# Chunk attention and a gelu MLP in one kernel: two more indices with a second block of seven products, totals of both halves in one set, and another order of mm1's steps

## The chip, the cores and the metric

The kernel runs on one core of a Trainium2 chip. A core has TensorE (matrix products, called PE in a profile, with its weight loads as PEld), VectorE (DVE), ScalarE (ACT), GpSimd (POOL) and SyncE (SP, which here only issues DMAs). Each engine takes its instructions in the order in which the program lists them for it, and waits where a semaphore is not there yet. Matrix products go from SBUF to PSUM, which has eight banks. The metric is the device time of one execution in microseconds.

## The reference

Attention is done within chunks of 64 keys, and its result is the input of a two-layer MLP with an exact gelu. Sizes: 8 batches, 8 heads, 576 positions, 64 per head; 4608 tokens, width 512, inner width 2048.

```python
scores = scale * np.matmul(q_c, k_c.transpose(0, 1, 2, 4, 3))     # per chunk of 64
attn = np.exp(scores - max) / (sum + 1e-09)
x = (attn @ v_c) ...transposed to (B * S, H * D)                   # 4608 x 512
h = x @ w_in                                                       # 512 x 2048
g = 0.5 * h * (1.0 + erf(h / sqrt(2)))
out = g @ w_out                                                    # 2048 x 512
```

## The kernel before

**Tiling.** The rows are cut into nine tiles of 512, called indices 0 to 8 (`t` in the code, `NT = 9`). Index t below 8 holds the first eight chunks of batch t; index 8 holds the ninth chunk of all batches. The loop `for t in range(1, NT)` does, in `phase(t, ...)`, the MLP of index t, and in between the attention of index n = t + 1, and starts that of index t + 2. `mm1` is x times w_in with the gelu; `mm2` is the product with w_out.

**mm1.** Its output, h, has 16 row blocks (128 inner columns of w_in each, 512 tokens wide). A *slot* makes one of them: four 128x512 matmuls (L463) into one bank of the pool `ps_mm`, and a gelu on ScalarE (L465). Four row blocks together can also be made by *seven products* in place of eight (`seven_rows`): the 2x2 block product of (512 x 512) w_in with x is formed by Strassen's scheme in Winograd's form. A product is four 128x256 matmuls (L536), `p1` to `p7`. It needs sums of blocks of x (`x_sums`, VectorE, L519) and of w_in (`w_in_sums`, VectorE, L513; set 0 for row blocks 0 to 3, set 1 for 4 to 7). The combining steps are `s11` (ScalarE copies p1 from bank a to bank b, L549), p5's copy to SBUF (L548, `kept`), `s12` and `c22+` (VectorE adds, L540) and the gelus `c11`, `c12`, `c22` and p3's own (L544). Banks a, b and d are shared: p6, p7 and p3 write over bank a, which `s12` and `c22+` read. Indices in `TWICE` (5 to 8) make row blocks 4 to 7 in this way too; those steps carry a prime (`p1'`), have banks a and b in the pool `ps_tp`, and take bank b of the first block as their d. The order of steps, slots (numbers) and hooks of an index is a tuple written out by hand in `mm1_seven`.

**mm2.** `mm2_seven` makes the 512 x 512 output of an index by seven products of 32 matmuls 128x256 (L683). It needs sums of blocks of h on VectorE: S1, S2, S4 in two parts each (`g_sum`, L621), and S3 (L608). Hook `g0` does the first parts, `s3` the third sum, and the second parts stand in mm2's hook 0 and 2. S1 and S2 lie in the memory that holds the sums of x during mm1. The results of the products are kept by ScalarE (L645), completed by VectorE (`done`, L650) and stored by SyncE.

**Attention of the next index.** `quad_S` makes the scores (64 small matmuls, L237), ScalarE the exponentials (L244), `quad_av` the products with v (L327). Sums of the exponentials: for indices 3 and 4 by a TensorE product with ones (`quad_sums`), spread by ScalarE copies (`quad_over`) and VectorE transposes; for indices 5 to 8 by VectorE alone: `quad_part` (L254, L257), then totals over pairs of quadrants, reciprocals and transposes (`quad_total`, `quad_rc`; L283 to L293). `quad_x_plain` (L320) and `quad_x` (L334) scale the result and give x of the next index.

**k by chunk.** For the scores, k is transposed by a DMA (`flip`, L194, tile k_t), which SyncE issues in its queue between loads and stores, and then copied to another layout (`k_by_chunk`, L205, four copies to tile k_c, which has one buffer): on VectorE for indices 3, 4 and 5, on ScalarE for the later ones. Where these copies stand among VectorE's other work is given by the hook that they hang on. In index 2 (for index 3) it was in front of slot 10, in index 3 (for index 4) in front of slot 8; in index 3 a second set (for index 5) hangs on slot 15 and has to wait until the scores of index 4 have read the only buffer.

**Start.** Before the first data are there, TensorE runs matmuls on zeros: three of 128x512, and `pass_blocks(108)`, 108 products of 64x64 by 64x8 (L821).

Of the kernel before, what the change touches and what calls it, by code (L numbers as in the profile page):

```python
# [11 lines left out]
def kernel(  # L12
# [9 lines left out]
    nc = tc.nc  # L22
    P = 128
    f32 = mybir.dt.float32
# [4 lines left out]
    CH = 64  # L29
# [3 lines left out]
    G = H // 2  # L33
# [5 lines left out]
    NT = B + 1  # L39
# [21 lines left out]
    QD = P // G  # L61
# [27 lines left out]
    work = ctx.enter_context(tc.tile_pool(name="work", bufs=3))  # L89
# [158 lines left out]
    def quad_part(t, g2, c):  # L248

        st = tiles[t]  # L250
        if c == 1:
            st["part", g2] = work.tile([P, 2, NB // 2, 2, 2], f32, tag="part", name="part", bufs=2)
        pt = work.tile([P, NB // 2, 32, 2], bf16, tag="pt", name="pt", bufs=2)
        nc.vector.transpose(  # L254
            pt[:].rearrange("p n e u -> p (n e u)").bitcast(f32).rearrange("p (n e) -> p n e", e=32),
            st["pT", 2 * g2 + c][:].rearrange("p i c -> p (i c)").bitcast(f32).rearrange("p (n e) -> p n e", e=32))
        nc.vector.tensor_reduce(st["part", g2][:, c, :, :, 0], pt[:].rearrange("p n e u -> p n u e"),  # L257
                                axis=mybir.AxisListType.X, op=mybir.AluOpType.add)

    def quad_across(t):  # L260

        part = [tiles[t]["part", g2] for g2 in range(2)]
        for g2 in range(2):
            for s in range(G):
                o = s ^ 1
                PO(part[g2][QD * s:QD * (s + 1), :, :, :, 1], part[g2][QD * o:QD * (o + 1), :, :, :, 0])

    def quad_total(t, halves=range(2)):

        part = [tiles[t]["part", g2] for g2 in range(2)]  # L270
        if 0 in halves:
            tiles[t]["across"] = [work.tile([P, NB], f32, tag="across", name="across", bufs=2) for _ in range(2)]
        across = tiles[t]["across"]
        for g2 in halves:
            total, rb = (work.tile([P, 2, NB], f32, tag=nm, name=nm, bufs=2) for nm in ("total", "rb"))
            if t == T0 + 2:
                nc.vector.tensor_reduce(total[:], part[g2][:].rearrange("p c n u s -> p c (n u) s"),
                                        axis=mybir.AxisListType.X, op=mybir.AluOpType.add)
            else:
                for s in range(G):  # L280
                    a, b = (part[g2][QD * q:QD * (q + 1), :, :, :, 0].rearrange("p c n u -> p c (n u)")
                            for q in (s, s ^ 1))
                    nc.vector.tensor_tensor(total[QD * s:QD * (s + 1)], a, b, op=ADD)  # L283
            nc.vector.reciprocal(rb[:, 0], total[:, 0])
            tiles[t]["rb", g2] = rb[:, 0], across[g2][:]
            if g2 == 0:
                quad_rc(t, 0, 0)
            for r in range(2):
                nc.vector.reciprocal(across[g2][CH * r:CH * (r + 1)], total[CH * (1 - r):CH * (2 - r), 1])  # L289

    def quad_rc(t, g2, c):
        rc = work.tile([P, NB, 32], f32, tag="rc", name="rc", bufs=4)
# [129 lines left out]
    NB = MT // 32  # L422
# [44 lines left out]
    NQ = 4  # L467
    T0 = 3
    DENSE = (0, 1)
    TWICE = range(T0 + 2, NT)  # L470

    HF = FF // 2
    HD = d_model // 2
# [87 lines left out]
    def mm1_seven(t, hooks):  # L561

        tiles[t]["h"] = hpool.tile([P, FF, MT], bf16, tag="h", name="h")
        kept = stage_tile()[:].rearrange("p (i f n) -> p i f n", f=HM, n=HD)
        bank, more = {}, {}
        does = seven_rows(t, 0, {"a": AT, "b": AT, "d": AT}, kept[:, 0], bank)
        if t in TWICE:
            does.update((step + "'", do) for step, do in
                        seven_rows(t, 1, {"a": TP, "b": TP}, kept[:, 1], more).items())
            fifth = does["p5'"]  # L570
            does["p5'"] = lambda: (more.update(d=bank["b"]), fifth())
        if t == NT - 1:
            order = ("p1", "s11", "p1'", "s11'", "p5", 8, "p2", "c11", "p6", 9, "s12", "p5'", "p6'", "s12'", 10, "p7", "p4",
                     "c22+", "c12", "c22", "p7'", 11, "p3", "p2'", "c11'", "c22+'", "p4'", "c22'", 12, "c12'", "p3'", 13,
                     "g0", 14, "s3", 15)
        elif t in TWICE:
            order = ("p1", "s11", "p5", 8, "p2", "p1'", "t0", "c11", "s11'", 9, "p5'", "p6", 10, "p6'", 11, "s12", "p7",
                     "s12'", "p7'", "p4", "c12", "c22+", "c22+'", "p2'", "c11'", "p4'", "t1", "c22", 12, "p3", "p3'",
                     "c12'", "c22'", 13, "g0", 14, "s3", 15)
        elif t == T0 + 1:  # L580
            order = ("x", 4, 5, 6, "p1", "s11", 7, "p5", "p2", "c11", "p6", 8, "s12", "t0", 9, "p4", "p7", "c12", "c22+", "t1",
                     10, "c22", 11, "p3", 12, "s3", 13, "g0", 14, 15)
        elif t == T0:
            order = ("x", "p1", "s11", 4, "p5", "p2", "c11", 5, "p6", "s12", 6, "p4", "p7", "c12", "c22+", 7, "c22", 8, "p3",
                     9, 10, "s3", 11, 12, 13, "g0", 14, 15)
        else:
            order = ("x", 4, 5, 6, "p1", "s11", 7, "p5", "p2", "c11", 8, "p6", "s12", 9, "p4", "p7", "c12", "c22+", 10, "c22",
                     11, "p3", 12, "s3", 13, "g0", 14, 15)
        for step in order:
            if step in does:  # L590
                does[step]()
                continue
            for u in hooks.get(step, ()):
                u()
            if not isinstance(step, str):
                mm1_slot(t, step)
# [232 lines left out]
    with tc.manual_schedule():  # L829
# [4 lines left out]
        win = [load_w_in(c, 2) for c in range(NWC - 1)]  # L834
        act_table(Act.Exp)
        keep_warm(3)
        pass_blocks(108)
        zero_k(k_bds[0], nc.gpsimd)
        zero_k(k_bds[1], nc.gpsimd)
        zero_v(0, nc.vector)  # L840
# [114 lines left out]
        for t in range(1, NT):  # L955
# [40 lines left out]
            if t <= T0:  # L996
# [2 lines left out]
                e2 = {0: [exp, lambda: quad_S(n, ALONE)] + g[1][:2], 2: g[1][2:],  # L999
                      4: [lambda: quad_sums(n)], 5: [ov[0]], 6: [ov[1]],  # L1000
                      7: [ov[2]] + rx[0], 8: [ov[3]] + rx[1], 9: rx[2], 10: rx[3]}
                e2[7 if t == 1 else 4].insert(1, lambda: quad_av(n, ALONE))
                if t > 1:
                    e1["x"] = [lambda: x_sums(t)]
                if t == 2:
                    e1[13] = [lambda: w_in_sums(1)]
                if t == 1:
                    e2[3] = [w_in_sums]
                    for i, f in ((1, 6), (2, 7), (3, 8), (4, 9)):
# [1 line left out]
                    e2[4].append(lambda: [load_qk(4, nm) for nm in "qk"])  # L1011
                    e2[7] += [lambda: pool_cast_qk(4), lambda: flip_qk(3), lambda: load_v_rows(3), lambda: cast_v_rows(3, PO)]
                else:
                    e1[10 if t < T0 else 8] = [lambda: k_by_chunk(n, DV)]
                if t < T0:
                    if t > 1:
                        e2[0].append(lambda: flip_qk(n + 1))
# [7 lines left out]
            elif n < NT:  # L1025
# [3 lines left out]
                    e1["t0"] = [lambda: quad_total(n, (0,))]  # L1029
                    e1["t1"] = [lambda: quad_total(n, (1,)), rcs[1]]  # L1030
                else:
                    e1["t0"] = [lambda: quad_total(n)]
                    e1["t1"] = rcs[1:]
                e2 = {0: [exp, lambda: quad_av(n, ALONE)] + xs[:2] + g[1][:2], 4: xs[2:] + g[1][2:],
                      6: [lambda: x_sums(n, (0, 1))], 10: [lambda: x_sums(n, (2, 3))], 11: [gelu]}
                if t == T0 + 1:
                    e2[0] = e2[0][:2] + g[1][:2] + xs[:2]
                    e2[2] = rcs[2:]
                if n + 1 < NT:
                    for i, gs in enumerate(((0,), (1, 2), (3,))):  # L1040
# [32 lines left out]
```

## Time and profile before

| | us |
|---|---|
| median of 3 runs (lowest, highest) | 275.51 (275.08, 276.24) |
| profiled execution | 275.01 |
| its span, first to last instruction | 273.2 |
| TensorE, VectorE, ScalarE, GpSimd busy | 263.5, 204.8, 192.8, 89.9 |
| index 2 (mm1 and mm2), from 78.72 to 106.85 | 28.1 |
| index 3, from 106.85 to 135.52 | 28.7 |
| index 4, from 135.52 to 163.04 | 27.5 |
| index 5, from 163.04 to 190.21 | 27.2 |
| index 6, from 190.21 to 217.45 | 27.2 |
| index 7, from 217.45 to 243.60 | 26.2 |

The times of the indices are starts of matmul rows in the trace. In a row of the timeline the first number is the start in us from the span's start, the second the length of the merged stretch, then engine, line and operation with its tiles (out<-in) and shapes, and in brackets the idle time in front and what ended it. Tile names can mislead: memory is shared, so that sums of h appear as `k_bd`, the second set of weight sums as `w_in_more` and the first as `w_out_sb`, and the SBUF copy of p5 as `arrival`.

### The profile page before, as it was taken

The numbers are of one execution on the slowest core, as the hardware profiler recorded it, in microseconds if no ns is written. First come the engines' busy times: TensorE is split into PE (matmuls) and PEld (weight loads), VectorE is DVE, ScalarE is ACT, GpSimd is POOL, SyncE is SP. The second block draws the span as 40 slices with busy tenths as digits, with TensorE's granted clock in tenths as the row PEclk, the third lists the DMA queues.
The fourth block names the chain that finished last, engine by engine and source line by source line (L and its number), as shares of the span: only waits on it lengthen the run. The fifth ranks groups of instructions, "written<-read, shape, count | busy, mean of one in ns | idle before, by whom it ended". The sixth has DMA issues, their size and how long they took to land. (4 is left out here: it accounts for less than half of the span.)

```text
span 273.2 us, 7277 instructions
## 1 busy us (share of the span) xinstructions
PE 263.5 (96%) x2911; PEld 184.2 (67%) x2933; DVE 204.8 (75%) x365; ACT 192.8 (71%) x372; POOL 89.9 (33%) x150
## 2 busy tenths in 40 slices
PE   7799999999999999999999999999999999999993
PEld 4564455546876687558755896688668866887683
DVE  5784457899883998669998999978997899724621
ACT  3767758888757867777877966897689769357710
POOL 7778768501383334105435800034100200000000
PEclk9999999999999999999999999999999999999999
DMA  6999999899999799999699327999973220130014
GB/s 192 265 341 402 395 397 233 233 243 245 339 321 222 211 327 141 299 265 267 176 255 339 72 79 191 169 139 164 238 167 89 89 79 0 41 106 12 1 42 115
DMA packets 104739, 53.97 MB, mean 198 GB/s; under 512 B 72960, under 2 KB 101632, under 8 KB 104704
## 3 DMA queue, kind: packets, MB, share of 16 engines
q1 hardware_dynamic: 104400, 53.23, 73.9%
q8 instruction: 23, 0.38, 0.6%
q10 hardware_dynamic: 304, 0.26, 0.3%
q14 instruction: 12, 0.10, 0.1%
HBM read 36.70 MB, written 9.44 MB: 169 GB/s over the span
## 5 line engine op out<-in xcount | busy, mean ns | idle before, releaser
L463 PE MATMUL h_ps<-x,w_in_sb 128*128 128x512 bf16 x356 | 85.5, 379 | 0.8
L465 ACT ACTIVATE h<-h_ps 128x512 bf16<-128x512 f32 x93 | 54.8, 600 | 23.4 <-PE h_ps L463 20.7
L463 PEld LDWEIGHTS <-w_in_sb 128*128 128x128 bf16 x372 | 36.4, 98 | 35.3 <-DVE w_in_sb L799 0.2
L164 POOL CAST q_nat<-arrival 128x512 bf16<-128x512 f32 x31 | 21.6, 736 | 58.6 <-DMA arrival<-in_q_dram 58.6
L683 PEld LDWEIGHTS <-h 128*128 128x128 bf16 x384 | 37.0, 98 | 5.0 <-issue 0.3
L212 POOL CAST v_nat<-arrival 128x1024 bf16<-128x1024 f32 x14 | 15.3, 1097 | 45.9 <-DMA arrival<-in_v_dram 28.8
L683 PE MATMUL y_ps<-v_bd,k_bd 128*128 128x256 bf16 x256 | 29.6, 273 | 0.1
L683 PE MATMUL y_ps<-w_out_sb,h 128*128 128x256 bf16 x256 | 29.3, 273 | 0.0
L683 PEld LDWEIGHTS <-k_bd 128*128 128x128 bf16 x256 | 24.8, 98 | 3.4 <-DVE w_out_sb L513 0.2
L650 DVE TENSOR_TENSOR kept<-y_ps,kept 128x512 f32<-128x512 f32 (+1 forms) x25 | 16.4, 656 | 12.6 <-PE y_ps L683 12.6
L827 ACT ACT_TABLE_LOAD x18 | 23.1, 1283 | 1.0 <-PEq L1057 0.7
L645 ACT COPY kept<-y_ps 128x512 f32<-128x512 f32 (+1 forms) x26 | 14.4, 555 | 11.3 <-PE y_ps L683 11.1
L164 POOL CAST k_nat<-arrival 128x512 bf16<-128x512 f32 x30 | 19.2, 673 | 9.6 <-DMA arrival<-in_k_dram 5.8
L544 ACT ACTIVATE h<-hs_ps 128x512 bf16<-128x512 f32 x33 | 18.5, 600 | 3.4 <-PE hs_ps L536 3.4
L540 DVE TENSOR_TENSOR hs_ps<-hs_ps,arrival 128x512 f32<-128x512 f32 x11 | 7.3, 685 | 12.0 <-PE hs_ps L536 10.8
L536 PEld LDWEIGHTS <-w_in_sb 128*128 128x128 bf16 x132 | 12.9, 98 | 4.5
L621 DVE TENSOR_TENSOR k_bd<-h 128x1024 bf16<-128x1024 bf16 x16 | 13.3, 834 | 3.1 <-ACT h L465 3.1
L683 PE MATMUL y_ps<-v_bd,h 128*128 128x256 bf16 x128 | 15.3, 272 | 0.2 <-DVE kept L650 0.2
L683 PE MATMUL y_ps<-v_bd,s_sb 128*128 128x256 bf16 x128 | 15.3, 273 | 0.0
L683 PE MATMUL y_ps<-w_out_sb,s 128*128 128x256 bf16 x128 | 15.3, 273 | 0.0
L244 ACT ACTIVATE pT<-s_ps 128x512 bf16<-128x512 f32 x28 | 14.4, 604 | 0.2 <-PE s_ps L237 0.2
L536 PEld LDWEIGHTS <-w_out_sb 128*128 128x128 bf16 x112 | 10.9, 97 | 5.1 <-issue 1.8
(132 smaller groups left out, 453.8 us busy)
## 6 DMA issues: line engine op xcount, KB each, us to landing
arrival<-in_v_dram SPq DMA_DIRECT2D x58, 128.0 KB, 4.3
arrival<-in_q_dram SPq DMA_DIRECT2D x7, 1024.0 KB, 7.4
arrival<-in_k_dram SPq DMA_DIRECT2D x6, 1024.0 KB, 9.7
out_dram<-kept SPq DMA_DIRECT2D x21, 256.0 KB, 2.6
arrival<-in_moe_w_out_dram SPq DMA_DIRECT2D x4, 1024.0 KB, 12.2
arrival<-in_moe_w_in_dram SPq DMA_DIRECT2D x6, 512.0 KB, 6.2
out_dram<-y_sb SPq DMA_DIRECT2D x11, 256.0 KB, 2.7
arrival<-in_k_dram SPq DMA_DIRECT2D x8, 256.0 KB, 6.3
```

The lines of the kernel that those rows point to most:

```text
L164: copy(st[nm][:, g].rearrange("p j r d -> p r j d"), st[nm + "f"][:, 2 * g:2 * g + 2])
L212: copy(st["v"][:, r::2], st["vf"][:, r::2])
L244: nc.scalar.activation(pT[:].rearrange("p u (c j) -> p u c j", j=J), s_ps[g2][c][:].rearrange("p u (j c) -> p u c j", j=J), Act.Exp, scale ...
L463: nc.tensor.matmul(h_ps[:], w_in_sb[:, ks, f * P:(f + 1) * P], tiles[t]["x"][:, ks, :], start=(ks == 0), stop=(ks == KS - 1))
L465: nc.scalar.activation(tiles[t]["h"][:, f, :], h_ps[:], Act.Gelu)
L536: nc.tensor.matmul(hs[:, f], left[:, ks, f * P:(f + 1) * P], right[:, ks], start=(fresh and f == 0 and ks == 0), stop=(ks == 1), skip_grou ...
L544: nc.scalar.activation(h[:, n:n + HM, HD * c:HD * (c + 1)], src, Act.Gelu)
L621: nc.vector.tensor_tensor(st["S", i][part], a, b, op=op)
L645: nc.scalar.copy(kept[name][:, ms], ps[:])
L650: nc.vector.tensor_tensor(y_sb[:, ms], ps[:], y_sb[:, ms], op=ADD)
L683: nc.tensor.matmul(to, left(f, m), right[:, f], start=(fresh and (split or m == 0) and f == 0), stop=(f == HF - 1), skip_group_check=True)
L827: nc.scalar.activation(act_scratch[:], rest[:, 0:1], func)
```

## The change

Three things are edited, and one number.

1. `TWICE` now holds 2, 3 and 5 to 8: indices 2 and 3 also make row blocks 4 to 7 by seven products. `w_in_sums(1)`, which index 2 did at slot 13, moves to a hook `w` in front of `s12`.
2. For indices 6 to 8 the totals of both halves are made in one set of VectorE instructions (`quad_totals`): four adds in place of eight, three reciprocals in place of six, and the transposes as they were. Index 5 keeps its reduce.
3. The order of mm1's steps is new in indices 2 to 7. The copies to k_c hang on a hook `k`: in index 2 behind p5', in index 3 behind p5. In index 3 s3 goes to the end of mm1; in index 4 p2 goes ahead of p5, and p3 and s3 go behind slots 11 and 12. In indices 5 to 7 p1' follows p1. In mm2, `quad_av` of index 2 moves to hook 5 and of index 3 to hook 6, and from index 5 on the first two x products stand behind the second parts of S1 and S2.
4. `pass_blocks(94)` in place of 108.

```diff
     def quad_part(t, g2, c):
...
-        if c == 1:
-            st["part", g2] = work.tile([P, 2, NB // 2, 2, 2], f32, tag="part", name="part", bufs=2)
+        if "part" not in st:
+            st["part"] = work.tile([P, 2, 2, NB // 2, 2, 2], f32, tag="part", name="part", bufs=2)
...
+    def quad_totals(t):
+
+        part = tiles[t]["part"]
+        total, rb = (work.tile([P, 2, 2, NB], f32, tag=nm, name=nm, bufs=2) for nm in ("total", "rb"))
+        for s in range(G):
+            a, b = (part[QD * q:QD * (q + 1), :, :, :, :, 0].rearrange("p c g n u -> p (c g) (n u)") for q in (s, s ^ 1))
+            nc.vector.tensor_tensor(total[QD * s:QD * (s + 1)].rearrange("p c g n -> p (c g) n"), a, b, op=ADD)
+        nc.vector.reciprocal(rb[:, 0], total[:, 0])
+        for g2 in range(2):
+            tiles[t]["rb", g2] = rb[:, 0, g2], rb[:, 1, g2]
+        quad_rc(t, 0, 0)
+        for r in range(2):
+            nc.vector.reciprocal(rb[CH * r:CH * (r + 1), 1], total[CH * (1 - r):CH * (2 - r), 1])
...
-    TWICE = range(T0 + 2, NT)
+    TWICE = (2, T0, *range(T0 + 2, NT))
...
-        elif t in TWICE:
-            order = ("p1", "s11", "p5", 8, "p2", "p1'", "t0", "c11", "s11'", 9, "p5'", "p6", 10, "p6'", 11, "s12", "p7",
-                     "s12'", "p7'", "p4", "c12", "c22+", "c22+'", "p2'", "c11'", "p4'", "t1", "c22", 12, "p3", "p3'",
-                     "c12'", "c22'", 13, "g0", 14, "s3", 15)
+        elif t > T0 + 1:
+            order = ("p1", "p1'", "s11", "t0", "s11'", 8, "p2", "p2'", "c11", "p5", "p6", "p5'", "p6'", "c11'", "s12", 9, 10,
+                     "s12'", "p7", "p4", "c22+", "p7'", "c22+'", "t1", "p4'", "c12", "c22", "p3", 11, "c12'", "c22'", 12, "p3'",
+                     13, "g0", 14, "s3", 15)
         elif t == T0 + 1:
-            order = ("x", 4, 5, 6, "p1", "s11", 7, "p5", "p2", "c11", "p6", 8, "s12", "t0", 9, "p4", "p7", "c12", "c22+", "t1",
-                     10, "c22", 11, "p3", 12, "s3", 13, "g0", 14, 15)
+            order = ("x", 4, 5, 6, "p1", "s11", 7, "p2", "p5", "c11", "p6", 8, "s12", "t0", 9, 10, "p4", "p7", "c12", "c22+",
+                     "t1", 11, "c22", 12, "p3", "s3", 13, "g0", 14, 15)
         elif t == T0:
-            order = ("x", "p1", "s11", 4, "p5", "p2", "c11", 5, "p6", "s12", 6, "p4", "p7", "c12", "c22+", 7, "c22", 8, "p3",
-                     9, 10, "s3", 11, 12, 13, "g0", 14, 15)
+            order = ("p1", "p1'", "s11", 8, "x", "p2", "c11", "s11'", "p6", "p5", "k", 9, "p5'", 10, "s12", "p6'", "s12'", 11,
+                     "p7", "p4", "c12", "p4'", "c12'", "p2'", "c22+", "c11'", "c22", "p7'", "p3", "c22+'", 12, "p3'", "c22'",
+                     13, "g0", 14, 15, "s3")
         else:
-            order = ("x", 4, 5, 6, "p1", "s11", 7, "p5", "p2", "c11", 8, "p6", "s12", 9, "p4", "p7", "c12", "c22+", 10, "c22",
-                     11, "p3", 12, "s3", 13, "g0", 14, 15)
+            order = ("p1", "p1'", "s11", "x", "s11'", 8, "p2", "p5", "p6", "c11", "p2'", "c11'", 9, 10, "w", "s12", 11, "p7",
+                     "p5'", "k", "p4", "c12", "c22+", "c22", "p6'", 12, "s12'", "p3", "p7'", "c22+'", "p4'", "c12'", "c22'",
+                     13, "p3'", 14, 15, "g0", "s3")
...
-        pass_blocks(108)
+        pass_blocks(94)
...
-                e2[7 if t == 1 else 4].insert(1, lambda: quad_av(n, ALONE))
+                e2[{1: 7, 2: 5, T0: 6}[t]].insert(1, lambda: quad_av(n, ALONE))
...
-                if t == 2:
-                    e1[13] = [lambda: w_in_sums(1)]
...
-                    e1[10 if t < T0 else 8] = [lambda: k_by_chunk(n, DV)]
+                    e1["w"] = [lambda: w_in_sums(1)]
+                    e1["k"] = [lambda: k_by_chunk(n, DV)]
...
-                    e1["t0"] = [lambda: quad_total(n)]
+                    e1["t0"] = [lambda: quad_totals(n)]
...
-                e2 = {0: [exp, lambda: quad_av(n, ALONE)] + xs[:2] + g[1][:2], 4: xs[2:] + g[1][2:],
+                e2 = {0: [exp, lambda: quad_av(n, ALONE)] + g[1][:2] + xs[:2], 4: xs[2:] + g[1][2:],
```

## The prediction

> **What bounds the kernel now.** I read the page's busy table and engine slices first, then the list of stages (one window for each index), then the queues in order of time around the steps that move. TensorE is busy 96% of the span and the granted clock is full, so a change is worth what it removes from TensorE's row, plus the gaps that it closes, less the gaps that it opens.
>
> ```profile
> PE 263.5 (96%) x2911; PEld 184.2 (67%) x2933; DVE 204.8 (75%) x365; ACT 192.8 (71%) x372; POOL 89.9 (33%) x150
> ...
> 78.70:106.85 28.15, 27.87 (x320) 19.56 (x321) 21.78 (x34) 20.49 (x46) 13.16 (x20) 1.00 0.97 242
> 106.85:135.50 28.65, 28.52 (x384) 20.07 (x384) 21.27 (x37) 22.56 (x50) 8.15 (x11) 1.00 1.00 239
> ...
> 163.00:190.20 27.20, 27.02 (x328) 20.64 (x329) 24.12 (x49) 21.72 (x36) 4.86 (x8) 1.00 0.98 166
> ```
>
> The columns of a window are its length, then busy time of PE, PEld, DVE, ACT and POOL, the clock, the DMA share. In indices 2 and 3 (first two windows) DMA is at 0.97 and 1.00: what SyncE's queue brings there comes at a time that TensorE's order does not set. Index 5 (third) has VectorE at 24.1 of 27.2 us.
>
> The second look is at who hands what to whom in index 3: SyncE's transpose of k, VectorE's copies of it, and the sums that TensorE waits for.
>
> ```profile
> 82.51 2.02 SPq L194 DMA_TRANSPOSE k_t<-k_nat  x1
> ...
> 108.98 1.91 SPq L194 DMA_TRANSPOSE k_t<-k_nat  x1
> ...
> 112.48 0.69 DVE L540 TENSOR_TENSOR arrival<-hs_ps,arrival 128x512 f32<-128x512 f32 x1 [1.18 <-PE hs_ps L536]
> 113.09 2.14 DVE L205 COPY k_c<-k_t 128x512 bf16<-128x512 bf16 x4
> 115.41 1.23 DVE L608 TENSOR_TENSOR s_sb<-h 128x2048 bf16<-128x2048 bf16 x1 [0.18 <-ACT h L544]
> ...
> DMA to landing us min/median/max: 3.9/3.9/4.1
> ```
>
> The last line (of the view of tile k_t) says 3.9 us from issue to landing: the k of index 3 lands at 82.51 + 3.9 = 86.4, that of index 4 at 108.98 + 3.9 = 112.9. The copies to k_c start at 87.54 and 113.09, just behind; nobody waits.
>
> ```profile
> 121.35 2.15 DVE L205 COPY k_c<-k_t 128x512 bf16<-128x512 bf16 x4 [1.33 <-PE s_ps L237]
> 123.40 0.69 DVE L621 TENSOR_TENSOR k_bd<-h 128x1024 bf16<-128x1024 bf16 x1
> 124.13 0.69 DVE L621 TENSOR_TENSOR k_bd<-k_bd,h 128x1024 bf16<-128x1024 bf16 x1
> ...
> 169.08 1.26 DVE L540 TENSOR_TENSOR hs_ps<-hs_ps,arrival 128x512 f32<-128x512 f32 x2
> ...
> 169.80 0.60 PE L536 MATMUL hs_ps<-k_bd,w_out_sb 128*128 128x256 bf16 x4
> ```
>
> The first three rows are VectorE held by scores of index 4, then the S sums of mm2; the last two are the gap that index 5 pays for its late totals.
>
> **The change part by part.**
>
> **Seven for eight.** A 128x512 matmul starts 216 ns after the one before it, a 128x256 one 109 ns (the median start distances of rows L463 and L683). Four slots are 16 x 216 = 3.46 us, a second block of seven is 28 x 109 = 3.05. Saved 0.40 in index 2 and 0.40 in index 3: 0.81. The twelve more weight loads each (98 ns, row L536) lie under 109 ns matmuls; without that cover they would cost 1.2 us an index. Each index gets two more ScalarE copies (0.585) and two more VectorE adds (0.686); both engines have 6 us or more idle in these windows, and what a late add holds up is counted below.
>
> **Totals in one set.** VectorE's stretch from the first total to s12 takes 169.08 - 165.22 = 3.86 us. Now: four adds of 64 elements (row: 0.198 for 32; I take 0.23), one reciprocal of 128x32 (0.354, row L306), one transpose (0.71), two half reciprocals (at most 0.354 each): 2.7. That is 1.15 us less in indices 5, 6 and 7. TensorE's gaps that it closes: a row of four 128x512 ends 4 x 0.216 after its start, so 169.80 is 0.24 late; in the same way I find 0.16 at 170.39, 0.32 at 197.04, 0.16 at 197.63 and 0.13 at 224.53: 1.0 us. The new order there asks for s12 after eight products and three slots, 6.1 us into mm1; the totals start 2.2 in, so s12 and s12' end at 6.2. No new wait: -1.0. If VectorE is late all the same, 0 of it comes. With the two x products behind the S sums, x is 1.4 us later; mm2's scores ask for its banks 7 us on, and that covers it.
>
> **Step k in index 2.** The four copies move ahead of c22+, and VectorE is one queue. w_in_sums (4 x 0.42) and s12 are done by 83.3, then it waits for k until 86.44; copies to 88.63, c22+ to 89.25. TensorE reaches p3, which rewrites the bank that c22+ reads, after ten products and five slots: 78.72 + 4.36 + 4.32 = 87.40. It waits 1.9 us, and p7' 0.17 more for s12'. With 0.40 saved and the old 0.16 gap gone, mm1 ends 1.5 later. w_in_sums no longer stands in front of the S sums (1.7 us of VectorE), so gaps of 0.16 and 0.33 late in mm2 (103.03, 105.11) can close: index 3 starts 1.2 later, at 108.05.
>
> **Step k in index 3.** It now stands ahead of s12. k lands at 112.84, copies to 115.03, s12 to 115.65; p7 waits for it. TensorE is there after seven products and four slots: 108.05 + 6.51 = 114.56, a wait of 1.15. This end does not depend on index 2: from 115.70 seven products and four slots remain, so mm1 ends at 122.2 against 120.5, +1.7.
>
> **s3 in index 3.** It was done 4 us ahead of VectorE's wait for the scores; it now stands behind that wait and the k copies, in front of S1 and S2. S2 then ends 1.23 later against the scores, 5.55 us after they start. TensorE wants its second half after 0.64 + 3.49 + 0.44 + 0.44 = 5.0 us (the attention products, 0.67, no longer stand ahead). A wait of 0.55; 0.85 if GpSimd's casts slow the two sums as they do the third (0.98 for 0.69). I take 0.7. Index 4 starts 2.4 later, 1.2 of it new.
>
> **Index 4.** p2 ahead of p5 covers the 0.33 us for which p5 waited at 139.73. But p3 has three slots behind it, not four, so s3 and all behind it come 0.86 later; the last x ended at 157.37, inside the scores that start at 157.11. Bounds 0 and 0.98; I take 0.9. Together +0.6.
>
> **At no cost.** quad_av later in indices 2 and 3: x asks for it 2 us after. SyncE's flips and loads and GpSimd's casts keep their order and are behind DMA; the flip and the loads at slot 9 of index 3 find SyncE still issuing what came before (110.98 to 113.21). Without that cover they move with the slot, under 2 us of transfers that nobody waits for. p1' right behind p1 would wait if it got the bank of mm2's last product: ScalarE's copy of that ends 0.79 after p1 starts, p1 takes 0.44, so 0.4 us in five indices, 2.0. Index 8 has this order already and starts at 243.60 with no gap; by that row I take 0.
>
> **pass_blocks.** 14 of 108 tiny products go, 1.61 x 14/108 = 0.2 us. They end at 4.0 and the next matmul waits for a cast of q until 4.46: no gain, and 0.2 lost at most if the wait were not there. The 128-column matmuls start 107 ns apart until 9.4 and 56 ns apart from 10.5 on, so the clock became full in between.
> The Trainium skill ("TensorE: Matmul & The Clock Gate", Part 1: The HAM clock gate) says that the array runs at half clock until a free-running window of about 3.4 us was busy; here the fast rows come 9 us after the first matmul, so these short bursts fill a window poorly, and by that rule a thinner start can bring the full clock a window later. By it the sum would be up to 1.4 us more, which is rival four.
>
> **Sum.** 1.2 + 1.2 + 0.6 - 1.0 = +2.0 us. The profiled execution took 275.0 (span 273.2, 1.8 around it); the three timed runs have a median of 275.5. I add to their mean, 275.25: 277.3.
>
> **The rivals.**
> One, faster: the k transposes land before they are asked for (by 84.5 and 111.7, so 1.9 and 1.1 us earlier) and the S sums keep up. Then 0.81, 1.0, 0.33 and the 0.5 of mm2's gaps in index 2 are all gained: -2.6, 272.6. For it: TensorE has that work less, and VectorE too. Against: SyncE's rows ahead of both transposes are back to back and DMA is full. It decides at 1.9 us.
> Two, no change: index 3's landing still costs 1.7, but the waits for S2 and x dissolve: 1.7 - 0.33 - 1.0 = +0.4, 275.7. For it: both waits are sums of short rows, each uncertain by a few tenths. Against: VectorE's row in mm2 of index 3 has no idle time of 0.5 us to take them up.
> Three, slower than forecast: VectorE's lateness is carried through index 4 and the totals win nothing back: 2.4 + 0.9 = +3.3, 278.6. For it: VectorE is at 89% in index 5. Against: it gets 1.15 us less there.
> Four: the clock. Were it half until 13.6, the last warming matmul, the stretch from 10.5 would double its 1.4 us of matmuls against 1.7 us of waits: 0 to 1.4 on top, 278.7 with the forecast. Against: the idle time in question grows from 0.45 to 0.65 us, and gaps of 0.4 to 0.5 at 5 to 8 us did not hinder the clock.
>
> **How the numbers follow.** Forecast 0.60, two 0.15, one 0.12, three 0.09, four 0.04. What a measurement tells from no change is 0.5%, 1.4 us. The forecast's own range is 276.1 (S2 and x at their lower bounds) to 278.3, and 0.08 of its 0.60 lies under 276.9. So slower 0.52 + 0.13 = 0.65, same 0.08 + 0.15 = 0.23, faster 0.12. A range from 274.6 to 279.2 leaves out most of the faster case and the end of the slow one.
>
> **What would show it.** Right: VectorE idle before the k copies of indices 2 and 3 for some 3 us, ended by the DMA; a TensorE gap near 1.9 us in index 2 and 1.1 in index 3, ended by L540; a gap in mm2 of index 3 ended by L621; no gap ended by L540 in indices 5 to 7. Wrong: copies of k with no wait ahead of them, or the prologue longer than 18.6 us.

## The result, and the profile after

The changed kernel takes 280.2 us (median of six runs, 278.0 to 283.7) against 275.8 beside it: 1.0134 times the time before, 95% interval 1.0092 to 1.0176. Medians are over all runs; ratios leave out slow runs, those over 1.5% above the fastest of their kernel (here 283.7). The forecast was 277.3, in a range from 274.6 to 279.2. The sign was right and the size too small: the prediction's sum is +2.0 us, and the medians differ by 4.4.

Line numbers of the changed kernel are 5 to 7 higher: what was L536, L540, L608, L621, L650 and L683 is now L541, L545, L615, L628, L657 and L690.

The profiled execution took 279.98 us (span 278.1, 4.9 longer). The page's busy line, and the windows of indices 2, 3 and 5:

```profile
PE 264.9 (95%) x2943; PEld 187.0 (67%) x2943; DVE 204.7 (74%) x348; ACT 195.4 (70%) x376; POOL 92.4 (33%) x150
...
79.42:108.01 28.59, 27.59 (x335) 20.70 (x333) 23.35 (x36) 21.28 (x48) 14.54 (x20) 1.00 1.01 250
108.01:139.94 31.93, 29.71 (x398) 21.90 (x396) 25.00 (x39) 23.16 (x52) 9.68 (x10) 0.95 0.77 198
168.19:194.95 26.76, 26.76 (x330) 20.63 (x328) 23.12 (x42) 22.05 (x36) 2.67 (x4) 1.00 1.02 140
```

Index 5 has no idle time on TensorE and is 0.4 us shorter, as forecast. Index 3 is 3.3 us longer (31.93 for 28.66), and its mean clock is 0.95. What happens there stands in the timeline, VectorE and GpSimd first, then TensorE, then a window of the stretch behind its wait:

```profile
122.05 2.99 DVE L205 COPY k_c<-k_t 128x512 bf16<-128x512 bf16 x4 [1.83 <-PE s_ps L237]
124.96 1.63 DVE L615 TENSOR_TENSOR s_sb<-h 128x2048 bf16<-128x2048 bf16 x1
126.52 1.09 DVE L628 TENSOR_TENSOR k_bd<-h 128x1024 bf16<-128x1024 bf16 x1
127.64 0.98 DVE L628 TENSOR_TENSOR k_bd<-k_bd,h 128x1024 bf16<-128x1024 bf16 x1
...
122.95 4.11 POOL L164 CAST q_nat<-arrival 128x512 bf16<-128x512 f32 x4 [15.50 <-DMA arrival<-in_q_dram]
127.02 3.65 POOL L164 CAST k_nat<-arrival 128x512 bf16<-128x512 f32 x4
...
128.68 2.74 PE L690 MATMUL y_ps<-v_bd,k_bd 128*128 128x256 bf16 x12 [2.17 <-DVE k_bd L628]
...
128.60:132.00 3.40, 3.32 (x68) 2.30 (x72) 2.96 (x6) 1.26 (x5) 3.40 (x5) 0.52 0.27 60
```

TensorE's wait for the second half of S2 is there, but it is 2.33 us by the start distances where 0.7 was forecast. In front of it the copies, s3, S1 and S2 take 2.99, 1.63, 1.09 and 0.98; undisturbed the same rows are 2.15, 1.23, 0.69 and 0.69. And GpSimd casts q and k of index 6 all the while; in the kernel before these casts started only as S2 ended:

```profile
124.63 2.79 POOL L164 CAST q_nat<-arrival 128x512 bf16<-128x512 f32 x4 [14.26 <-DMA arrival<-in_q_dram]
```

Behind the wait the granted clock is 0.52: twelve products in 2.74 us.

The k copies of indices 2 and 3, and what waits behind them:

```profile
86.41 2.14 DVE L205 COPY k_c<-k_t 128x512 bf16<-128x512 bf16 x4 [1.05 <-DMA k_t<-k_nat]
...
89.20 0.60 PE L541 MATMUL hs_ps<-k_bd,w_in_sb 128*128 128x256 bf16 x4 [0.94 <-DVE arrival L545]
...
111.82 2.14 DVE L205 COPY k_c<-k_t 128x512 bf16<-128x512 bf16 x4 [2.21 <-DMA k_t<-k_nat]
113.88 1.28 DVE L545 TENSOR_TENSOR hs_ps<-hs_ps,arrival 128x512 f32<-128x512 f32 x2
```

Both sets wait for the DMA. p3 in index 2 loses 1.10 us (start distances), p7 in index 3 only 0.1. And the totals, in indices 5 and 6:

```profile
170.36 0.91 DVE L288 TENSOR_TENSOR total<-part 32x64 f32<-32x64 f32 x4
...
196.87 2.29 DVE L288 TENSOR_TENSOR total<-part 32x64 f32<-32x64 f32 x4
...
196.79 2.29 POOL L164 CAST k_nat<-arrival 128x512 bf16<-128x512 f32 x4 [5.83 <-DMA arrival<-in_v_dram]
...
201.66 0.60 PE L541 MATMUL hs_ps<-k_bd,w_out_sb 128*128 128x256 bf16 x4 [0.46 <-DVE hs_ps L545]
```

The four adds take 0.91 as costed, or 2.29 when a cast of k runs beside them; then p7 is late again, by 0.62.

### The profile page after: what moved, and what is told of

Read it like the earlier page. It is cut to its first block, busy times and chain, and to the rows that moved or that the text cites. A ratio compares the mean times of both kernels' runs of the same rounds, so it can differ in the third digit from the quotient of the medians.

```text
span 278.1 us, 7304 instructions
## 1 busy us (share of the span) xinstructions
PE 264.9 (95%) x2943; PEld 187.0 (67%) x2943; DVE 204.7 (74%) x348; ACT 195.4 (70%) x376; POOL 92.4 (33%) x150
## 5 line engine op out<-in xcount | busy, mean ns | idle before, releaser
L468 PE MATMUL h_ps<-x,w_in_sb 128*128 128x512 bf16 x340 | 79.3, 379 | 0.0
L470 ACT ACTIVATE h<-h_ps 128x512 bf16<-128x512 f32 x85 | 50.5, 599 | 17.5 <-PE h_ps L468 16.7
L468 PEld LDWEIGHTS <-w_in_sb 128*128 128x128 bf16 x340 | 33.3, 98 | 32.9 <-DVE w_in_sb L806 0.2
L690 PEld LDWEIGHTS <-h 128*128 128x128 bf16 x384 | 37.0, 98 | 4.7
L690 PE MATMUL y_ps<-v_bd,k_bd 128*128 128x256 bf16 x256 | 31.4, 280 | 2.4 <-DVE k_bd L628 2.2
L690 PEld LDWEIGHTS <-k_bd 128*128 128x128 bf16 x256 | 25.2, 100 | 7.0 <-DVE k_bd L628 2.8
L690 PE MATMUL y_ps<-w_out_sb,h 128*128 128x256 bf16 x256 | 29.3, 273 | 0.0
L164 POOL CAST k_nat<-arrival 128x512 bf16<-128x512 f32 x30 | 21.7, 758 | 12.1 <-DMA arrival<-in_v_dram 5.8
L657 DVE TENSOR_TENSOR kept<-y_ps,kept 128x512 f32<-128x512 f32 (+1 forms) x25 | 16.4, 657 | 12.2 <-PE y_ps L690 9.0
L549 ACT ACTIVATE h<-hs_ps 128x512 bf16<-128x512 f32 x39 | 22.8, 599 | 2.8 <-PE hs_ps L541 2.7
L652 ACT COPY kept<-y_ps 128x512 f32<-128x512 f32 (+1 forms) x26 | 14.5, 556 | 12.5 <-PE y_ps L690 12.3
L541 PEld LDWEIGHTS <-w_in_sb 128*128 128x128 bf16 x156 | 15.3, 98 | 6.5 <-issue 1.4
L628 DVE TENSOR_TENSOR k_bd<-h 128x1024 bf16<-128x1024 bf16 x16 | 12.1, 758 | 5.2 <-ACT h L470 5.1
L690 PE MATMUL y_ps<-v_bd,s_sb 128*128 128x256 bf16 x128 | 15.3, 273 | 0.0
L690 PE MATMUL y_ps<-w_out_sb,s 128*128 128x256 bf16 x128 | 15.3, 273 | 0.0
L690 PE MATMUL y_ps<-v_bd,h 128*128 128x256 bf16 x128 | 15.3, 272 | 0.0
L319 ACT COPY rb<-r 32x16 f32<-32x16 f32 x48 | 9.7, 202 | 7.8 <-DVE r L311 7.2
L628 DVE TENSOR_TENSOR k_bd<-k_bd,h 128x1024 bf16<-128x1024 bf16 x16 | 12.1, 758 | 2.9 <-PE hs_ps L541 2.1
```

The lines of the kernel that those rows point to most:

```text
L164: copy(st[nm][:, g].rearrange("p j r d -> p r j d"), st[nm + "f"][:, 2 * g:2 * g + 2])
L468: nc.tensor.matmul(h_ps[:], w_in_sb[:, ks, f * P:(f + 1) * P], tiles[t]["x"][:, ks, :], start=(ks == 0), stop=(ks == KS - 1))
L470: nc.scalar.activation(tiles[t]["h"][:, f, :], h_ps[:], Act.Gelu)
L541: nc.tensor.matmul(hs[:, f], left[:, ks, f * P:(f + 1) * P], right[:, ks], start=(fresh and f == 0 and ks == 0), stop=(ks == 1), skip_grou ...
L549: nc.scalar.activation(h[:, n:n + HM, HD * c:HD * (c + 1)], src, Act.Gelu)
L628: nc.vector.tensor_tensor(st["S", i][part], a, b, op=op)
```

## The experiments

All executions vary in the start, so the stages are compared. Each column of the table is the time from one set of scores to the next in the trace of one execution; the first is where those of index 1's mm2 start, "3, mm2" is what lies between the two sets in index 3's mm2, the last but one goes to the end. The forecast row is the prediction's terms, put into these columns. Each ratio in the text is against runs of the kernel before on the same chip; their medians are 275.8 to 276.2.

| kernel | start | 2 | 3, mm1 | 3, mm2 | 4 | 5 | 6 | 7, 8 | median us |
|---|---|---|---|---|---|---|---|---|---|
| before | 64.52 | 27.86 | 28.14 | 10.76 | 25.83 | 27.21 | 27.24 | 61.67 | 275.8 |
| forecast | 64.5 | 29.4 | 28.3 | 11.5 | 25.5 | 27.7 | 26.8 | 61.5 | 277.3 |
| changed | 65.22 | 28.57 | 27.43 | 14.57 | 25.73 | 27.53 | 27.38 | 61.70 | 280.2 |
| s3_back | 67.00 | 29.67 | 27.32 | 11.16 | 25.98 | 27.53 | 26.98 | 61.84 | 277.2 |
| copies_late | 64.48 | 29.46 | 27.32 | 11.30 | 26.21 | 27.54 | 27.12 | 61.78 | 277.3 |
| filled | 64.23 | 29.32 | 27.32 | 13.17 | 25.99 | 27.53 | 26.77 | 61.71 | 278.2 |
| casts_held | 67.09 | 33.56 | 27.67 | 11.16 | 25.58 | 27.54 | 26.77 | 63.55 | 284.4 |
| casts_held_b | 65.54 | 31.33 | 27.32 | 11.17 | 25.70 | 27.53 | 27.34 | 61.71 | 279.3 |
| k_late | 66.01 | 27.31 | 28.63 | 11.86 | 25.87 | 27.53 | 27.76 | 61.70 | 278.3 |
| totals_only | 64.60 | 27.86 | 28.22 | 10.58 | 26.44 | 27.17 | 26.77 | 63.84 | 277.1 |
| totals_again | 64.43 | 27.86 | 28.15 | 10.58 | 26.29 | 26.92 | 26.79 | 63.57 | (276.8, one run) |
| s3_alone | 65.00 | 27.86 | 27.99 | 11.95 | 26.88 | 27.49 | 28.15 | 61.69 | (278.9, one run) |
| start_108 | 66.07 | 31.27 | 27.33 | 15.02 | 25.88 | 27.54 | 26.77 | 62.07 | (283.7, one run) |
| mended | 65.24 | 27.31 | 28.90 | 10.80 | 25.97 | 27.23 | 27.66 | 61.78 | 276.9 |
| mended_2 | 64.47 | 27.31 | 30.20 | 11.28 | 40.96 | 26.77 | 26.77 | 61.54 | 292.9 |
| mended_3 | 65.74 | 27.31 | 27.33 | 11.17 | 25.53 | 27.37 | 26.77 | 61.72 | 273.8 |

The theory at the start is this: the wait for S2 comes from what stands in front of S1 and S2 on VectorE, slowed by GpSimd's casts, and brings the half clock with it. The rival: VectorE has too much to do there in any order.

**s3 ahead of the copies again.**

```diff
-                     13, "g0", 14, 15, "s3")
+                     13, "g0", 14, "s3", 15)
```

> The changed kernel with one step moved: in index 3 s3 stands ahead of slot 15 again, so ahead of VectorE's wait for the scores and of the k copies. Theory (the order of VectorE's queue: what stands behind that wait is late, and TensorE's 2.33 us wait is also what brings the half clock behind it): S2's second part ends about 1.6 us earlier (s3 took 1.63), the gap at the second half of the S2 product falls from 2.33 to about 0.7, no product behind it starts 213 ns after the last, and the 1.9 us of slow products go too: 3.5 us less than the changed kernel, about 276.5. Rival (VectorE has too much to do in mm2 of index 3; a wait taken away there comes back at the next sum, x or store): the gap falls, but the start of index 4's attention products moves by under 1 us, about 279.5.

1.0056 times the time before (1.0022 to 1.0090). mm2 of index 3 takes 11.16, 3.4 less, and the wait is 0.35. Index 4 gives back 0.25 of it (25.98 for 25.73), with a wait of 0.31 for the sums of x. The theory holds as to the order, and the rival falls; the casts are not tested here.

**The second set of k copies behind S4.**

```diff
-                    e1[15] = [lambda: k_by_chunk(n + 1, DV)]
...
+                    e2[2].append(lambda: k_by_chunk(n + 1, DV))
```

> The changed kernel with one hook moved: in index 3 the k copies for index 5 stand behind the second part of S4 in mm2, and no longer ahead of s3 and S1. VectorE then does not wait for the scores before the sums. Theory: S1 and S2 end near 123, ahead of TensorE's want at 126.3; the gap of 2.33 and the half clock behind it go, 4.2 us less, about 276.0; the copies end some 4 us later, still ahead of the scores of index 5 at 132. Rival (VectorE's total work sets the end): x of index 4 comes later by the copies' 2.2 us and index 4 gives back half or more, 278 or above.

1.0043 (1.0014 to 1.0072); mm2 of index 3 takes 11.30. No wait for S2 is left, only 0.43 for a copy of ScalarE and 0.30 for x. Of the 1.3 us by which the median misses 276.0, 0.9 lie in index 2, which waits 1.99 at p3 here and 1.10 in the changed kernel's profile. Which of the two things in front of S1 goes does not matter.

**The casts held back until S2 is done.** GpSimd first copies one element of S2, and so starts the casts of index 6 behind it; the loads stay at their hook.

```diff
+            def held_casts():
+                PO(gate[:], tiles[t]["S", 2][1][:, 0, 0:1])
+                pool_cast_qk(t + 3)
+                cast_v_rows(n + 1, PO)
...
+                    e2[0].append(held_casts)
```

> The changed kernel, but GpSimd's casts of q and k of index 6 and of v of index 5 wait for S2's second part (one element of it is read by GpSimd first). Theory A (the casts beside VectorE made k copies, s3, S1 and S2 slower: 2.99, 1.63, 1.09, 0.98 where 2.15, 1.23, 0.69, 0.69 were seen without them): these durations come back, S2 ends 1.9 us earlier, the gap falls from 2.33 to about 0.4 to 0.7, as predicted from the undisturbed rows, and the half clock goes: about 276.5. Theory B (the order alone makes the wait; the casts beside it are a coincidence): durations stay near 3.0, 1.6 and 1.0 and the gap stays over 1.8.

In mm2 of index 3 all came as theory A says (11.16), but the run as a whole took 1.0331 times the time before (1.0247 to 1.0414): index 2, which the edit does not touch, took 33.56. (At the scores of index 8 it also waited 1.8 for ScalarE's copies of k.) The only thing that the edit changes for index 2 is a new tile of two bytes. So the same again without the tile, with the element put into `rest[:, 511:512]`:

> As the run with the casts held, but the one element that GpSimd reads is written to a column of the zero tile that nothing reads later, and there is no extra tile of two bytes in SBUF. If the tile's two bytes, by shifting what lies behind it, made the DMA of that run late (index 2 took 33.6 there, and k of index 3 landed at 91.6 where the others had 86.2 to 89), index 2 takes 28.6 to 29.7 as in the other runs and the time is about 277.5. If holding the casts did it, it stays near 284. In index 3 the sums should take 0.69 again and the S2 gap should be 0.35, in both cases.

1.0109 (1.0075 to 1.0143). VectorE's rows in index 3's mm2, and TensorE's:

```profile
125.02 2.14 DVE L205 COPY k_c<-k_t 128x512 bf16<-128x512 bf16 x4 [1.83 <-PE s_ps L237]
127.08 1.22 DVE L615 TENSOR_TENSOR s_sb<-h 128x2048 bf16<-128x2048 bf16 x1
128.21 0.69 DVE L628 TENSOR_TENSOR k_bd<-h 128x1024 bf16<-128x1024 bf16 x1
128.93 0.69 DVE L628 TENSOR_TENSOR k_bd<-k_bd,h 128x1024 bf16<-128x1024 bf16 x1
...
129.68 1.48 PE L690 MATMUL y_ps<-v_bd,k_bd 128*128 128x256 bf16 x12 [0.20 <-DVE k_bd L628]
```

The order is that of the changed kernel. Without the casts beside them all four steps have the durations that the prediction used, the wait is 0.36 by start distances (forecast 0.55 to 0.85), and there is no half clock. So order alone makes some 0.4 us, and the casts the rest. Four executions have this order of S1, S2 and what stands in front of them, with TensorE's wait left as it is, and differ in when the casts start: 1.12 us behind the first scores of mm2 (start_108, below), 1.73 (the changed kernel), 3.61 (k_late, below) and 6.14 here. The waits are 2.76, 2.33, 1.05 and 0.36. The whole time does not show it, because index 2 waits 2.45 us and then has the half clock (31.33). Whether the tile cost anything is not settled: the four runs with it took 283.1 to 287.4, the four without 278.1 to 279.7, but they ran on another chip, and index 2 is late in runs without it too (31.33 here, 31.27 in start_108).

**TensorE's wait filled.** Eleven products on zeros where the wait is:

```diff
+                    if t == T0 and s == 2 and m == 0 and f == HF // 2:
+                        early.append(ps_mm.tile([P, HM, HD], f32, tag="mm", name="y_ps"))
+                        for _ in range(11):
+                            nc.tensor.matmul(early[0][:], rest[:, 0:P], rest[:], start=True, stop=True)
```

> The changed kernel with eleven matmuls 128x512 on zeros (0.216 each, 2.4 us) put where TensorE waits in index 3, ahead of the second half of the S2 product; they write a bank that is cleared before use. Nothing else moves. Theory (the 2.33 us of idle time made the clock fall): the products behind start 109 ns apart and not 213, the mean granted clock is 0.999, and the stretch from S2's end to the attention products is 1.9 us shorter: 278.1 at the most, 2 less than the changed kernel. Rival (these products are slow because of what they read, beside VectorE's and GpSimd's writes): the spacing stays 213 ns and the time stays at 280.

1.0101 (1.0067 to 1.0134). These are the added products, and the twelve behind them:

```profile
126.00 2.54 PE L693 MATMUL y_ps<-rest 128*128 128x512 bf16 x11
128.38 1.47 PE L694 MATMUL y_ps<-v_bd,k_bd 128*128 128x256 bf16 x12
```

1.47 us for the twelve and not 2.74. mm2 takes 1.40 less (13.17), with the wait still there: that is what the half clock cost, a little less than the 1.9 expected. It was the idle time, not the operands: the same twelve products run at full speed here.

**s3 alone, in the kernel before.**

```diff
-                     9, 10, "s3", 11, 12, 13, "g0", 14, 15)
+                     9, 10, 11, 12, 13, "g0", 14, 15, "s3")
```

> The kernel before with one step moved: s3 of index 3 to the end of mm1, behind the k copies for index 5. By the rows of before (k copies end at 123.45, s3 1.23, two sums 0.69 to 0.98) S2's second part ends at 126.0 to 126.6, and TensorE asks for it at 126.2: a gap of 0 to 0.5, index 3's mm2 (scores to scores, 10.76 before) up to 11.3, and no half clock. If s3's place alone made the 2.33 us, without casts of GpSimd beside it, mm2 takes 12.5 or more.

mm2 of index 3 takes 11.95: more than the order's 0.5, less than 12.5. In this execution the casts started at 123.52, under s3 (1.64) and S1 (1.09), and S2 is 0.92 late; index 4 adds 1.05, waiting for the sums of x and for x. So a cost of s3's place was right in kind in the prediction, and its size goes with the time at which the casts start; these wait for the transfer that brings q of index 6.

**k later.** In index 2 `"k"` goes from behind p5' to behind c22+', in index 3 from behind p5 to behind s12'.

> The changed kernel with the hook k alone moved back: in index 2 behind c22+', in index 3 behind s12'. Theory: in index 2 nothing of the second set waits behind the landing of k, so the gap at p3 (1.10 in the changed kernel's profile, 1.8 to 2.2 in the three runs beside it) and the 0.17 behind it go, and index 2, from scores to scores, takes 27.6 (28.6 to 29.7 with the hook in front). In index 3 p7's wait of 0.1 goes. The wait for S2 in index 3 stays, with its half clock. About 278.6. Rival (the copies are late wherever they stand, and the sums of mm2 in index 2 inherit it): a gap ended by L628 of 1 us or more comes up in index 2's mm2, and index 2 stays above 28.6.

1.0079 (1.0052 to 1.0106). Index 2 falls to 27.31, and stays there in every run with k behind: the hook in front costs all of index 2's wait. 0.39 and 0.31 come back in its mm2 (L628, L657) and 0.62 at p3 of index 3, whose c22+ now stands behind the copies; less than the rival's 1 us. The wait for S2 in index 3 is 1.05 in this execution, without a half clock, where 2.33 with one was expected to stay: the casts came later.

**The totals alone.** Indices 2 to 4 and the start as before; `quad_totals`, the orders of indices 5 to 7 and the x products as in the change.

> The kernel before with the second part of the change alone: totals of both halves in one set, the new order in indices 5 to 7, the x products behind the S sums, the one tile for the parts. Indices 2 to 4 and the start are as before. Theory (as predicted): the gaps at p7 and p7' of indices 5 to 7 (1.0 in all) go, where no cast of GpSimd runs beside the four adds: 274.8, and 275.4 where one does. Rival (later x or a bank of p1' costs as much as the totals save): no change, 275.8, with a gap ended by L339 in a later index.

1.0045 (1.0021 to 1.0069), slower than before, where a gain of 1.0 us was expected. Indices 5 to 7 did gain it: no gap is left at p7 or p7'. But index 4 is 0.6 longer, and 2.2 us come at the very end. The same kernel, profiled once more for the open part:

> A second profile of the second part alone. In the first one indices 5 to 7 gained the 1.0 us as predicted, but index 4 was 0.6 longer (p5 0.93 late for the sums of x, 0.40 for x of index 5) and the last ScalarE store was issued in 2.74 us where before took 0.73, 2.2 us at the end. If the end is chance, it is at 61.7 from the last scores again and the time is near 275.4; if the part brings it, it is at 63.8 again. If index 4's 0.6 comes from GpSimd's casts over S2 and S4 of index 3 (1.13 and 0.98 for 0.69), it goes where those sums take 0.69.

Both come again, 0.46 in index 4 and 1.9 at the end. At the end ScalarE issues one store in 2.49 us (0.73 before and in the changed kernel), and all behind it is late:

```profile
267.71 2.49 ACTq L707 DMA_DIRECT2D out_dram<-kept  x1
```

It came in both profiles of that build, so it is hardly chance; why, the trace does not say, and the changed kernel does not have it. For index 4 the second profile agrees with the casts over S2 and S4 (0.98 each, casts from 123.51), but no run of this kernel took them away, so that cause is not shown.

**108 tiny products again.**

```diff
-        pass_blocks(94)
+        pass_blocks(108)
```

> The changed kernel with 108 tiny products at the start, as before. If the thinner start costs the 0.70 us that the changed kernel's profile lost before 18.8, or holds back the clock, the first scores of index 3 start at 64.5 or less. If the loads' landing sets the start (64.2 to 67.1 in nine profiles with 94 products, 64.5 and 64.6 in two with 108), it falls anywhere in that range and the time is 278 to 280.5.

The scores of index 1's mm2 (they are index 2's; the expectation calls them index 3's) start at 66.07, later than the changed kernel's 65.22. So fourteen more products do not bring the early start back. In the changed kernel GpSimd's cast of the last part of k waited for its load until 11.47, before until 10.77, as much as the 0.70; in this run it started at 10.82, so other things delay the start too, and they were not followed up. The run is 3 us above what was expected, since index 2 took 31.27 with a half clock and mm2 of index 3 15.02.

**Mended by order.** k late as above, the second k copies behind S4, and in index 4 `"c22", "p3", 12` for `"c22", 12, "p3"`.

> The change with its three costs taken out by order alone: k behind c22+' in index 2 and s12' in index 3; the k copies for index 5 behind S4's second part; in index 4 p3 ahead of slot 12. Theory (each wait is a matter of who stands in front on VectorE): no gap over 0.4 in indices 2 to 4; index 2 27.6, index 3 as in the run with late copies, x of index 5 in time: 273.5 to 274.5, faster than the kernel before. Rival (VectorE's work in indices 2 to 4 does not fit any more with four more adds): the gaps move on to the S sums or x, and it stays at 276 or above.

1.0032 (1.0006 to 1.0057): a miss, by the waits that k_late also had (0.66 and 0.31 in mm2 of index 2, 0.62 at p3 of index 3), and 0.90 at p7 of index 6, where the totals took 2.57 beside a cast. Four edits were made against these waits:

> The mended version with four more edits, each for a gap that its profile still had: in index 2 two of the four k copies stand behind s12', the other two behind c22+' (gaps of 0.66 and 0.31 in mm2); in index 3 k stands behind p5 as in the change (0.62 at p3); in index 4 two of the four partial sums stand behind the sums of x (0.34 at p5); in indices 5 to 7 slot 11 stands ahead of p7 (0.90 in index 6, where a cast of GpSimd held up the totals). Theory (all of it is order on VectorE): index 2 and mm1 of index 3 together 54.7 to 55.2 (56.2), index 6 26.8 (27.7), 274.4, faster than the kernel before by 0.4 to 0.8%. Rival (x of index 5 is held up by VectorE's total work in index 4, and what TensorE gains ahead of it is waited for there): 275.5 to 276, no change.

1.0594 (1.0545 to 1.0643). The edit in index 4 was a mistake. It moved GpSimd's exchange of the partial sums behind the casts in GpSimd's queue, which wait for a load, and VectorE waited 13.70 us for it with all that stood behind. The other edits did what they should (27.31, 26.77). In index 3, with k in front and index 2 no longer late, p7 waits 2.88 us. TensorE arrives there at 112.50 and k lands at 112.61, so the copies and s12 behind the landing are paid in full:

```profile
115.38 0.60 PE L541 MATMUL hs_ps<-k_bd,w_out_sb 128*128 128x256 bf16 x4 [2.72 <-DVE hs_ps L545]
```

**The k copies in two pairs.**

```diff
-                     "p5'", "k", "p4", "c12", "c22+", "c22", "p6'", 12, "s12'", "p3", "p7'", "c22+'", "p4'", "c12'", "c22'",
+                     "p5'", "p4", "c12", "c22+", "c22", "p6'", 12, "s12'", "k0", "p3", "p7'", "c22+'", "k", "p4'", "c12'", "c22'",
...
+                    e1["k0"] = [lambda: k_by_chunk(n, DV, (0, 1))]
+                    e1["k"] = [lambda: k_by_chunk(n, DV, (2, 3))]
```

> The mended version with two edits of mended_2 kept and one made new: the k copies stand in two pairs, behind s12' and behind c22+' in index 2, behind s12' and behind c22+ in index 3; slot 11 stands ahead of p7 in indices 5 to 7. The partial sums of index 5 and GpSimd's exchange of them are back in their old places, since behind GpSimd's casts the exchange came 13 us late. Theory: index 2 takes 27.3 with no gap in its mm2 and mm1 of index 3 27.4 (k copies wait for nothing that TensorE waits for), 54.7 together against 56.0 before and 56.2 in the mended version; mm2 of index 3 10.8 to 11.3; index 4 26.0 with 0.3 to 0.5 for x; index 6 26.8. About 274.5, faster than before by 0.4 to 0.8%. Rival (k of index 4 lands at a time of its own, and whatever stands behind its copies waits): a gap of 1 us or more in mm1 of index 3, 275.5 to 276.

273.8 us, 0.9925 times the time before (0.9898 to 0.9952). No wait of TensorE over 0.5 us is left in indices 2 to 7. Against before the columns give -0.55, -0.81, +0.41, -0.30, +0.16, -0.47 and +0.05: -1.5 in one execution; the medians differ by 2.1.

## Why the prediction was right and wrong

**Seven for eight, -0.40 an index: right.** Index 2 without a wait is 27.31 against 27.86, which is 0.40 and the old gap of 0.16. The column of index 3's mm1 without a wait is 27.32 against 28.14: 0.40, 0.16, and a net 0.26 in the end of index 2's mm2, where the old gaps of 0.16 and 0.33 are gone.

**Step k in index 2, p3 waits 1.9: right.** 1.80, 1.99 and 2.19 in three executions with the same code up to there; 1.10 in the profiled one, since k was there 0.7 us sooner after the index began. What was missing is its spread: 1.10 to 3.53 over seven executions, with a half clock behind the wait in three of them.

**Step k in index 3, p7 waits 1.15: too large here.** The wait is the landing less TensorE's arrival, as the prediction had it. TensorE came as forecast, 6.5 us after the index began, but k landed at 111.80 and not at 112.84, and 1.15 - 1.04 is the 0.1 seen. Its transpose was issued at 106.50 in place of 108.98 and took 5.3 us to land in place of 3.9, so the landing was no fixed time, as the sum had it. Nor could the wait be left out: it is 2.88 in mended_2.

**s3 in index 3's mm2, a wait of 0.7: the step that failed.** It came to 3.8 us (14.57 for 10.76): 2.33 of waiting and 1.4 of half clock. The mechanism, place and releaser were right; the size failed in two ways, the casts (some 2 us) and the clock. The durations were read from rows that no cast ran beside, and only S1 and S2 were given a slower value; but the change puts s3 9.5 us later and S1 and S2 3 us later, while the casts come 1.7 us earlier (122.95 for 124.63), over the end of the k copies too. Without the casts the same order waits 0.36. And the clock was weighed as a rival for the start only, not behind each wait that the sum itself contained.

**Index 4, +0.6: right.** It is 28.25 against 27.53 from start to start: p5 no longer waits (0.33), 0.27 goes to S2, 0.76 to x.

**Totals, -1.0: right but for one index.** Indices 5 to 7 are 0.40, 0.47 and 0.13 shorter where no cast runs beside the adds (the run with the filled wait), just the gaps listed. In the changed kernel's profile index 6 gave back 0.62, and in four other executions 0.35 to 0.99.

**At no cost.** No run shows a cost of `pass_blocks`: the first column is 64.23 to 67.09 with 94 products and 64.43 to 66.07 with 108. p1' right behind p1 was right: there is no gap there in any run. GpSimd's casts "keep their order and are behind DMA": true, and the wrong question, since it is what runs beside them that pays.

**The rivals.** The third and the fourth (278.6 and 278.7) came nearest, both with the wrong place. The third's lateness of VectorE was not carried on but paid at once in mm2 of index 3. The fourth had the half clock at the start; there the clock was full from 9.0 us in the changed kernel's profile and from 10.1 before, and it fell in mm2 of index 3.

**The signs.** The waits of VectorE for k came, but are 1.05 and 2.21 us and not some 3. "None by L540 in indices 5 to 7" was wrong for index 6. The start was longer by 0.70 us in the profiled execution, which the prediction had named as a sign of being wrong; the late start of start_108 speaks against the number of products as its cause.

## What to carry to other kernels

When a step is moved, look at what the other engines run beside its new place, not only at what stands in front of it: a duration belongs to its neighbours too. Where a copy that waits for a DMA is put ahead of work that TensorE waits for, the time starts to vary with the transfer; put such copies behind that work, or split them, so that each piece fits an idle stretch. A wait of 2 us or more on TensorE can cost more in clock on top (1.4 us here), depending on when it falls.

## What was not expected of the hardware

**VectorE and GpSimd.** Side by side S1 and S2 took 1.09 and 0.98 where they take 0.69 alone, and a cast of q or k 1.06 where it takes 0.61 alone: both got longer. The four adds of the totals went from 0.91 to 2.29, one beside each cast, while the four casts kept the 2.29 that they also take without them. The Trainium skill ("SBUF — State Buffer", Who interferes with whom) says that a VectorE instruction with two SBUF inputs, or a copy in a fast mode, and a GpSimd instruction that reads SBUF shut each other out for a whole instruction. The trace agrees for the S sums and the k copies; for the totals only VectorE lost time. It says as well that a reduction does not contend: the reductions of index 6 take 0.69 beside the casts of s3_alone, as they do alone.

**The clock.** It fell to half at waits of 2.12, 2.33, 2.45, 2.76 and 3.53 us, and did not at 1.80, 1.99, 2.19 and 2.88. Here is one of each kind, p3 of index 2 in casts_held_b and in s3_back:

```profile
90.87 1.01 PE L541 MATMUL hs_ps<-k_bd,w_in_sb 128*128 128x256 bf16 x4 [2.29 <-DVE arrival L545]
```

```profile
92.07 0.60 PE L541 MATMUL hs_ps<-k_bd,w_in_sb 128*128 128x256 bf16 x4 [2.03 <-DVE arrival L545]
```

So length alone does not decide. The granted clock of the profile shows each of the five falls to last 3.41 us. The one of the changed kernel, with the stretches in front and behind (behind the length stand the busy times of PE, PEld, DVE, ACT and POOL, then the clock and DMA):

```profile
125.00:128.42 3.42, 1.46 (x13) 0.71 (x11) 3.38 (x4) 0.86 (x2) 3.42 (x4) 1.00 0.96 215
128.42:131.83 3.41, 3.15 (x48) 2.13 (x52) 2.98 (x6) 1.09 (x5) 3.41 (x5) 0.50 0.31 70
131.83:135.00 3.17, 3.17 (x72) 2.85 (x63) 2.95 (x5) 2.73 (x12) 0.81 (x1) 1.00 0.25 88
```

The other changes of the clock in a trace lie a whole number of 3.41 us away from its fall; a trace without a fall on the way has one behind the last matmul. If each trace is cut into stretches of 3.41 us from there, TensorE was idle (by start distances) for 2.2 to 2.6 us in the stretch ahead of each of the five falls. Behind stretches with 1.9 us or less no fall follows from index 2 on: the 2.88 of mended_2 is cut into 1.01 and 1.87, the 2.19 of s3_back into 1.26 and 0.93. This is read from the traces and was not tested by a run of its own. The Trainium skill ("TensorE: Matmul & The Clock Gate", Part 1) has a window of about 3.4 us that runs by itself, and the trace agrees. It lets the clock fall after an idle window; here windows that were idle for two thirds were enough.
